# First batch, first token tile: the channel mixer's first product of four channel pairs with plain blocks and a relu from PSUM

## The chip, the cores and the metric

The kernel runs on one core of one Trainium2 chip. The metric is the device time of one launch in microseconds (us). The kernel before took 2399.0 us, the median of three runs from 2398.49 to 2399.86.

Engines by the names of the profile: PE is TensorE (PEld its weight loads), DVE is VectorE, ACT is ScalarE, POOL is GpSimd, SP is SyncE. SP, ACT and POOL also issue DMAs.

## What is computed

For x of shape (8, 3008, 256), float32: a global filter over the sequence, then a token mixer and a channel mixer.

```python
X = np.fft.rfft(x, axis=1)
x = np.fft.irfft(X * (filt_r + 1j * filt_i), n=3008, axis=1)
h = np.maximum(x.transpose(0, 2, 1) @ w_tok1, 0.0) @ w_tok2     # w_tok1 (3008, 256), w_tok2 (256, 3008)
u = x + h.transpose(0, 2, 1)
out = u + np.maximum(u @ w_ch1, 0.0) @ w_ch2                    # w_ch1 (256, 1536), w_ch2 (1536, 256)
```

The four mixer weights come as 64-bit floats; the kernel loads their words and makes float32 of them on the chip.

## The kernel before, in words

**Order of the work.** All is written out by hand: each engine executes its instructions in the order in which the Python code issues them. The transform of batch 0 comes first, then the token product of batch 0, then the mixer. `mix` goes through 288 items, one for each batch b, token tile m (six tiles of 512 tokens, the last of 448) and channel pair jp (six pairs of 2 x 128 hidden channels). Between the parts of an item, the main loop issues the steps of the next batch's transform. In items 0 to 5 (batch 0, tile 0) those are the first products of batch 1's transform (`a_unit`, L532, called x products in what follows), whose results are copied by ACT (L541) and stored to z_tmp by ACT's DMA queue (L543).

**One item, up.** "Up" is u @ w_ch1 for one pair: a product of a 2 x 2 block matrix of weights with a 2 x 2 block matrix of u (two halves of 128 input channels, two halves of 256 tokens). It is done with Strassen's method in Winograd's form: seven products of 128x128 weights with 256 columns instead of eight. `up_first` (L968 on) issues four of the seven (L973) into two PSUM banks "pg" and ACT copies the first result to s (L976). `up_middle` makes two sums on DVE: hh (128x256) and s (128x512), each with one input from PSUM. `up_last` issues the other three products (L989), makes two sums of 128x512 into hh on DVE, and ACT applies relu to hh in place (L994). All DVE sums go through the helper `v` and so have the line L951. The right-hand sums of u that the method needs are the tile v, made by `v_steps`.

**One item, down.** "Down" is relu(...) @ w_ch2 for the pair of the item before, again with seven products (`down`, L1007), accumulated over the six pairs in four PSUM banks "po". Its sums of hh are the tile t (`h_sums`: a 128x512 and two 128x256 sums). Part 0 of it uses hh, parts 1 and 2 use t.

**The weights.** The seven weight blocks of each pair lie in a tile wc: chan[0] for w_ch1, chan[1] for w_ch2. A loaded piece of 128x512 words (`wc1_load`, L392, four DMAs; `wc2_load`, L403, one DMA) is made float32 in steps: ACT L281, DVE L283 and L284, then DVE L287, L289 and the sum L316 into wc. These five DVE steps are called a convert. The raw blocks are then in four of the seven places, and `combine` (L377 to L384) makes the other sums in place with five 128x128 operations on POOL, L380 to L384. The converts of the last ten pieces (the list LAST) are spread over items 0 to 5, one or two an item: wc2 0, wc1 1, wc1 4, wc2 1, wc1 2, wc2 2, wc1 5, wc2 3, wc2 4, wc2 5. A wc1 piece serves two pairs for one half of the input channels; with its second half there, `wc1_load` combines the first pair of the two at once and puts the second off until the next wc2 piece. The list `stages` gives these pieces four buffers in turn, so a piece's load waits for the convert four pieces earlier.

**What else stands in the queues.** POOL, after the last combines, clears three filter tiles (L587) for batch 1's transform and, from item 4 on, stores the token weights' raw blocks (`w1_sums`, L796 and L797). SP loads batch 1's remaining rows of x, then reads z_tmp back (L659, L660) and loads the filters (L227 to L233); their product is L705 on DVE. ACT issues the stores of z_tmp. In item 3, two token units of the next tile (`u_unit`, L880 and L872) are issued on PE.

The lines above are those of the kernel before; the diff adds lines, so that in the kernel after they stand 2 to 20 lines further down.

Of the kernel before, what the change touches and what calls it, by code (L numbers as in the profile page):

```python
# [13 lines left out]
AF = mybir.ActivationFunctionType  # L14
# [30 lines left out]
DH = D // P  # L45
# [4 lines left out]
W2G = -(-N2 // NG)  # L50
PARTS = (0, 64, 96, 112)
BY_PE = 6
AP = A // 2
W1S = 7
IN_B = 16
# [73 lines left out]
def kernel(  # L129
# [11 lines left out]
    nc = tc.nc  # L141
# [41 lines left out]
    def bank(tag):  # L183
        return (psg if tag == "pg" else psum).tile([P, 512], FP32, tag=tag, name="ps_" + tag)
# [30 lines left out]
    chan = []  # L215
# [172 lines left out]
    def wc1_load(i, late=True):  # L388
        c, q = divmod(i, DC // 512)
        st = stage(512)  # L390
        for g in range(CB):
            nc.gpsimd.dma_start(st[ts(g, CW)], moe_w_ch1[ds((g * DH + c) * CW, CW), ts(q, 512)])  # L392
        yield

        yield from rounded(st, 512, [(lambda v: v.rearrange("p (i j n) -> p i j n", j=2, n=P),
                           chan[0][:, 2 * q:2 * q + 2, slice(0, 5, 4) if c == 0 else slice(1, 7, 5)])], late)
        if c == DH - 1:
            combine(chan[0][:, 2 * q:2 * q + 1])
            put_off.append(2 * q + 1)

# [568 lines left out]
    def up_first(jp, ut, vt, w, g):  # L969
        hw = w // 2  # L970
        for ps, n, mov in ((g[0][:, 0], 0, ut[:, 0, 0:hw]), (g[0][:, 1], 5, vt[:, 2, 0:hw]),
                           (g[1][:, 0], 6, vt[:, 0, 0:hw]), (g[1][:, 1], 4, vt[:, 1, 0:hw])):
            nc.tensor.matmul(ps[:, 0:hw], chan[0][:, jp, n, :], mov, start=True, stop=True)  # L973

        s = sp.tile([P, 3, 256], FP32, tag="s", name="s")[:, :, 0:hw]
        nc.scalar.copy(out=s[:, 0], in_=g[0][:, 0, 0:hw])  # L976
        return s

    def up_middle(hh, w, g, s):
        hw = w // 2  # L980
        u2 = hh[:, 2, 0:hw]
        v(u2, g[0][:, 1, 0:hw], s[:, 0])
        v(s[:, 1:3], g[1][:, :, 0:hw], u2.unsqueeze(1).to_broadcast([P, 2, hw]))

    def up_last(jp, ut, vt, w, g, s, hh):
        hw = w // 2
        for ps, n, mov in ((g[0][:, 0], 1, ut[:, 1, 0:hw]), (g[0][:, 1], 2, ut[:, 1, hw:w]),
                           (g[1][:, 1], 3, vt[:, 3, 0:hw])):
            nc.tensor.matmul(ps[:, 0:hw], chan[0][:, jp, n, :], mov, start=True, stop=True)  # L989
        h = hh[:, :, 0:hw]  # L990
        for i, add in enumerate((s[:, 0:2], s[:, 2].unsqueeze(1).to_broadcast([P, 2, hw]))):
            hs = h[:, 2 * i:2 * i + 2]
            v(hs, g[i][:, :, 0:hw], add)
            nc.scalar.activation(out=hs, in_=hs, func=AF.Relu)  # L994
# [103 lines left out]
    h1s, uts, vts = {}, {}, {}  # L1098
# [6 lines left out]
    def v_steps(b, m):  # L1105
        vts[b, m] = vp.tile([P, 4, 256], FP32, tag="v", name="v")
        t13, t2, t4_ = u_sums(uts[b, m], vts[b, m], width(m))

        def t24():
            t2()  # L1110
            t4_()

        return [t13, t24]

    todo_v = []
# [5 lines left out]
    def mix(next_ready):  # L1121

        wait = []
        pos, hhs, tts = {}, {}, {}

        def loads(b):
            if b + 1 < B and next_ready(b):
                for c in wait:
                    t4_load(b + 1, c)
                wait.clear()  # L1130


        own = ({(3, 0): (0,), (3, 2): (1,)}, {(2, 2): (0,), (3, 0): (1,), (3, 2): (2, 3)})
        new = {(JP - 2, 0): (0, 1), (JP - 1, 0): (2, 3)}

        def u_parts(b, m, jp, place):
            parts = own[b > 0] if m + 1 < MT else new if b + 1 < B else {}
            now = parts.get((jp, place), ())
            b, m = (b, m + 1) if m + 1 < MT else (b + 1, 0)
            for part in now:  # L1140
                u_part(b, m, part)
            if now and now[-1] == max(p for ps in parts.values() for p in ps):
                if m:
                    wait.append(m)
                todo_v.extend(v_steps(b, m))
                if b and (b, m) < (B - 1, MT - 2):
                    w2m_load((m + 2) % MT)

        to_dram = [f for m in range(MT) for f in w2_sums(m)]
        w1_todo, w1_out = w1_sums()  # L1150
        items = [(b, m, jp) for b in range(B) for m in range(MT) for jp in range(JP)]
        n = MT * JP
        for i in range(len(items) + 1):
            now, old = i < len(items), i >= 1
            if not now:
                bo, mo, jo = items[i - 1]
                t = tp.tile([P, 4, 256], FP32, tag="t", name="t")
                last_item(bo, mo, jo, hhs.pop(i - 1), t, uts[bo, mo], pos[bo, mo])
                break
            if i == JP - 2:  # L1160
                w1_todo.pop(0)()
            elif JP + 2 <= i and w1_todo:
                for _ in range(2):
                    w1_todo.pop(0)()
            elif i > JP + 2 and w1_out:
                w1_out.pop(0)()
            if i and ended[0] < len(tiles):
                convert_middle()
                convert_end(False)
                convert_middle()  # L1170
            if now:
                b, m, jp = items[i]
                if i % n == 0:
                    wait.append(0)
                w = width(m)
                hhs[i] = hp.tile([P, 4, 256], FP32, tag="hh", name="hh")
                g = [bank("pg").rearrange("p (s n) -> p s n", s=2) for _ in range(2)]
                s = up_first(jp, uts[b, m], vts[b, m], w, g)
                up_middle(hhs[i], w, g, s)
            while todo_h1:  # L1180
                todo_h1.pop()()
            if i < JP:
                one_step()
            if old:
                bo, mo, jo = items[i - 1]
                tts[i - 1] = tp.tile([P, 4, 256], FP32, tag="t", name="t")
                for f in h_sums(hhs[i - 1], tts[i - 1], width(mo)):
                    f()
                down(mo, jo, 0, hhs[i - 1], tts[i - 1], pos.setdefault((bo, mo), []))
            if now:  # L1190
                u_parts(b, m, jp, 0)
            copies()
            yield b, i % n, 0
            if ended[0] < len(tiles):
                if i == 0:
                    convert_middle()
                convert_end(False)
            if now:
                up_last(jp, uts[b, m], vts[b, m], w, g, s, hhs[i])
                if b + 1 < B and i % n == n - 4:  # L1200
                    t4_sums(b + 1, 0)
            one_step()
            if i >= JP:
                one_step()
            if now and b + 1 < B:
                if n - 4 - W1S <= i % n < n - 4:
                    w1_load(i % n - (n - 4 - W1S))
                if i % n == n - 4:
                    t4_sums(b + 1, 1)
            copies()  # L1210
            loads(b)
            yield b, i % n, 1
            if old:
                down(mo, jo, 1, hhs[i - 1], tts[i - 1], pos[bo, mo])
            yield b, i % n, 1.5
            if old:
                down(mo, jo, 2, hhs.pop(i - 1), tts.pop(i - 1), pos[bo, mo])
                if jo == JP - 1:
                    todo_v.extend(finish(bo, mo, uts[bo, mo], pos[bo, mo]))
                    one_step()  # L1220
                    one_step()
            if now:
                if b + 1 < B and i % n == n - 4:
                    h1s[b + 1] = yield from token_product(b + 1)
                u_parts(b, m, jp, 2)
                if jp == JP - 1:
                    while todo_v and m + 1 == MT:
                        one_step()
                if i >= 8 and to_dram:
                    to_dram.pop(0)()  # L1230
                if i in (28, 29):
                    w2m_load(i - 28)
            loads(b)
            yield b, i % n, 2
        while todo_v:
            one_step()

    with tc.manual_schedule():
# [45 lines left out]
        for i in range(IN_B, A // 2 + TC * W2G):  # L1284
            convert()
            if i == A // 2 + BY_PE - 1:
                sum_up()
# [4 lines left out]
        for dh in range(DH):  # L1292
            convert()
            u_part(0, 0, dh)
        for f in v_steps(0, 0):
            f()
        convert_end(False)
        for _ in range(XB):
            next(second)
# [8 lines left out]
        n = MT * JP  # L1308
        for b, i, place in mix(next_ready):
# [12 lines left out]
            jp = i % JP  # L1322
# [44 lines left out]
```

## Time and profile before

| | us |
|---|---|
| median of the timed runs | 2399.0 |
| the profiled execution's own time | 2400.86 |
| its span, from the first to the last instruction | 2399.1 |
| start of item 0's up on PE | 141.8 |
| start of item 4's up on PE | 184.7 |
| mean granted TensorE clock | 0.994 |

How to read it: a row of a timeline has the start and the length in us, the engine, the line, the operation, the tile written and the tiles read, their shapes, and how many instructions were merged; in square brackets stands how long the engine was idle before it, and what ended that. A row of the windows has the stretch, its length, and the busy time of PE, PEld, DVE, ACT and POOL, each with a count, then the granted clock, the DMA engines' share and GB/s. The chain of waits lists start, length, engine, tile and line.

### The profile page before, as it was taken

What the parts mean: (1) busy time and instruction counts of PE and PEld (TensorE: products, weight loads), DVE (VectorE), ACT (ScalarE), POOL (GpSimd) and SP (SyncE); (2) the same over time, 40 slices, a digit from 0 to 9 for tenths busy, and PEclk for the clock granted to TensorE, in tenths of its full rate; (3) what the DMA queues carried; (4) which work ended last, traced back from release to release, by engine and by line L of the source; (5) the groups of instructions that cost most, each with busy time, mean ns of one, the idle gap of its engine ahead of it and who ended that gap; (6) DMA issues with size and microseconds to landing.
All of it is one profiled execution on the core that took longest, in us unless ns stands there. A gap on an engine that the chain in (4) does not pass through costs nothing.

```text
span 2399.1 us, 37048 instructions
## 1 busy us (share of the span) xinstructions
PE 2360.7 (98%) x13132; PEld 2014.8 (84%) x13132; DVE 1949.3 (81%) x3669; ACT 689.8 (29%) x1339; POOL 639.8 (27%) x1124
## 2 busy tenths in 40 slices
PE   7989999999999999999999999999999999999998
PEld 4667788888898888988888888988889888898887
DVE  7798887788887888788887788788888788877786
ACT  5732232222223222232222222132222322212222
POOL 7475624211211121112112311221121112112121
PEclk8999999999999999999999999999999999999999
DMA  8864446333354333533345333533335433331100
GB/s 225 238 188 125 149 130 223 121 109 89 109 181 128 101 98 110 194 114 99 96 149 158 113 94 103 188 118 107 92 114 172 135 96 98 108 130 32 39 15 21
DMA packets 190423, 294.28 MB, mean 123 GB/s; under 512 B 34444, under 2 KB 124962, under 8 KB 190238
## 3 DMA queue, kind: packets, MB, share of 16 engines
q1 hardware_dynamic: 148750, 231.24, 31.1%
q0 software_dynamic: 34688, 53.83, 8.6%
q10 hardware_dynamic: 6800, 6.85, 0.9%
q8 instruction: 104, 1.70, 0.3%
q14 instruction: 81, 0.66, 0.1%
HBM read 209.06 MB, written 82.72 MB: 122 GB/s over the span
## 4 chain that ended last, share of the span: by engine, by line
PE 92%; DVE 3%; DMA 3%; issue 1%; ACT 1%; POOL 1%; SPq 0%; ACTq 0%; DVEq 0%; POOLq 0%
PE ps_po L1007 35%; PE ps_pg L973 19%; PE ps_pg L989 15%; PE ps_b L525 3%; PE ps_b L837 3%; PE ps_acc L894 3%; PE ps_pg L525 2%; PE ps_acc L837 2%; PE ps_b L894 2%; PE ps_acc L872 2%; PE ps_b L872 2%; PE ps_b L786 1%; DMA x<-in_x_dram 1%; DMA filt<-in_filt_i_dram 1%; PE ps_acc L880 1%
## 5 line engine op out<-in xcount | busy, mean ns | idle before, releaser
L1015 POOL DMA_DIRECT2D out_dram<-r x752 | 408.2, 550 | 1451.2 <-issue 864.2
L994 ACT ACTIVATE hh<-hh 128x512 f32<-128x512 f32 (+1 forms) x576 | 347.7, 621 | 1002.1 <-DVE hh L951 998.3
L951 DVE TENSOR_TENSOR hh<-ps_pg,s 128x512 f32<-128x512 f32 (+3 forms) x864 | 481.9, 585 | 166.2 <-ACT s L976 156.1
L1007 PE MATMUL ps_po<-t,wc 128*128 128x256 f32 (+1 forms) x2296 | 556.4, 379 | 0.7 <-DVE t L951 0.6
L1007 PEld LDWEIGHTS ps_po<-t,wc 128*128 128x128 f32 x2296 | 427.1, 190 | 91.4 <-issue 33.5
L973 PE MATMUL ps_pg<-v,wc 128*128 128x256 f32 (+1 forms) x1728 | 413.6, 375 | 0.7 <-POOL wc L383 0.7
L1007 PE MATMUL ps_po<-hh,wc 128*128 128x256 f32 (+1 forms) x1722 | 411.5, 375 | 0.6 <-POOL wc L384 0.6
L973 PEld LDWEIGHTS ps_pg<-v,wc 128*128 128x128 f32 x1728 | 328.8, 190 | 39.0 <-POOL wc L383 1.2
L1007 PEld LDWEIGHTS ps_po<-hh,wc 128*128 128x128 f32 x1722 | 326.9, 190 | 38.5 <-POOL wc L384 1.4
L989 PE MATMUL ps_pg<-u,wc 128*128 128x256 f32 (+1 forms) x1152 | 291.8, 376 | 2.1 <-DVE hh L951 2.0
L951 DVE TENSOR_TENSOR t<-t,hh 128x256 f32<-128x256 f32 (+1 forms) x576 | 246.3, 428 | 19.8
L989 PEld LDWEIGHTS ps_pg<-u,wc 128*128 128x128 f32 x1152 | 216.9, 190 | 33.7 <-DVE hh L951 7.8
L951 DVE TENSOR_TENSOR s<-ps_pg,hh 128x512 f32<-128x512 f32 (+1 forms) x288 | 196.0, 681 | 30.0
L976 ACT COPY s<-ps_pg 128x256 f32<-128x256 f32 (+1 forms) x288 | 105.9, 368 | 331.1 <-PE ps_pg L973 329.9
L951 DVE TENSOR_TENSOR t<-hh 128x512 f32<-128x512 f32 (+1 forms) x288 | 194.3, 675 | 0.6 <-ACT hh L994 0.6
L973 PE MATMUL ps_pg<-u,wc 128*128 128x256 f32 (+1 forms) x576 | 170.0, 377 | 4.2 <-DVE hh L951 4.2
L989 PE MATMUL ps_pg<-v,wc 128*128 128x256 f32 (+1 forms) x576 | 168.8, 375 | 0.0
L973 PEld LDWEIGHTS ps_pg<-u,wc 128*128 128x128 f32 x576 | 107.9, 190 | 20.6 <-DVE hh L951 8.1
L989 PEld LDWEIGHTS ps_pg<-v,wc 128*128 128x128 f32 x576 | 108.9, 190 | 12.9
L951 DVE TENSOR_TENSOR u<-ps_acc,u 128x256 f32<-128x256 f32 (+1 forms) x84 | 46.1, 549 | 73.0 <-PE ps_acc L894 50.5
L951 DVE TENSOR_TENSOR u<-ps_b,u 128x512 f32<-128x512 f32 (+2 forms) x126 | 74.4, 591 | 28.9 <-PE ps_b L894 26.7
L894 PE MATMUL ps_acc<-w 128*128 128x256 f32 (+1 forms) x336 | 85.2, 376 | 0.0
(164 smaller groups left out, 2684.8 us busy)
## 6 DMA issues: line engine op xcount, KB each, us to landing
w<-w_tmp SPq DMA_DIRECT2D x84, 448.0 KB
w<-w_tmp SPq DMA_DIRECT2D x35, 896.0 KB
out_dram<-r POOLq DMA_DIRECT2D x696, 32.0 KB, 3.5
g_tmp<-t SPq DMA_DIRECT2D x112, 192.0 KB
t<-g_tmp SPq DMA_DIRECT2D x42, 512.0 KB
t<-z_tmp SPq DMA_DIRECT2D x196, 96.0 KB
z_tmp<-t SPq DMA_DIRECT2D x72, 256.0 KB
wb<-wbi_t SPq DMA_DIRECT2D x56, 256.0 KB
```

What stands on the lines that cost most here:

```text
L525: nc.tensor.matmul(outs(i, j), stat(i, j), mov(i, j), start=True, stop=True)
L786: nc.tensor.matmul(acc[:, t, :], w1[:, a, ts(t, P)], t4[b, a // TC4][:, a % TC4, :], start=(a == 0 and t == 0), stop=(a == A - 1 and t == ...
L837: nc.tensor.matmul(ps[:, at], w[:, n], mov, start=(j == 0 and i in (0, 2)), stop=(j == AP - 1 and i >= 5))
L872: nc.tensor.matmul(ps[:, ds(q * P, n)], t4[b, c][:, r, ts(dh, P)], wai[:, 0:n], start=(first and q == 0), stop=(not first and q == 3))
L894: nc.tensor.matmul(ps[:, ds(j * hw, hw)], h1[:, n, :], w2m[m % 2][:, at, 0:hw], start=(i < 2 and j == 0), stop=(j == len(todo) - 1))
L951: nc.vector.tensor_tensor(out=out, in0=in0, in1=in1, op=op)
L973: nc.tensor.matmul(ps[:, 0:hw], chan[0][:, jp, n, :], mov, start=True, stop=True)
L976: nc.scalar.copy(out=s[:, 0], in_=g[0][:, 0, 0:hw])
L989: nc.tensor.matmul(ps[:, 0:hw], chan[0][:, jp, n, :], mov, start=True, stop=True)
L994: nc.scalar.activation(out=hs, in_=hs, func=AF.Relu)
L1007: nc.tensor.matmul(po[i][:, j, 0:hw], chan[1][:, jp, n, :], mov, start=(jp == 0 and first == 1), stop=(jp == JP - 1 and last == 1))
L1015: q.dma_start(bass.AP(tensor=ob.tensor, offset=ob.offset + row * D + g * cw, ap=[[N1 * D, 32], [D if h else -D, n], [1, cw]]), blocks[ts(g ...
```

## The change

In the first four items (batch 0, tile 0, pairs 0 to 3) up is done with plain blocks: four products of 128x128 raw weights with 512 columns (`up_plain`), and ACT's relu reads the two PSUM banks and writes hh: one instruction of 128x512 for the first bank, two of 128x256 for the second, whose two halves go to hh in reversed order. No v, no s and no sums on DVE are used there. The combines of pairs 0 to 3 of w_ch1 leave the converts and are issued one an item in items 1 to 4, each behind the up of that item. The two v steps of tile 0, which stood ahead of the mixer, become steps that item 0 takes one by one.

```diff
+PLAIN = 4
...
-        if c == DH - 1:
+        if c == DH - 1 and 2 * q >= PLAIN:
             combine(chan[0][:, 2 * q:2 * q + 1])
             put_off.append(2 * q + 1)
...
+    def up_plain(jp, ut, hh):
+        ps = [bank("pg") for _ in range(2)]
+        for dh in range(DH):
+            for i, n in enumerate(((0, 4), (1, 6))[dh]):
+                nc.tensor.matmul(ps[i], chan[0][:, jp, n, :], ut[:, dh, :], start=(dh == 0), stop=(dh == 1))
+        for i in range(2):
+            two = ps[i].rearrange("p (s n) -> p s n", s=2)
+            if i == 0:
+                nc.scalar.activation(out=hh[:, 0:2], in_=two, func=AF.Relu)
+            else:
+                for j in range(2):
+                    nc.scalar.activation(out=hh[:, 3 - j], in_=two[:, j], func=AF.Relu)
...
                 hhs[i] = hp.tile([P, 4, 256], FP32, tag="hh", name="hh")
-                g = [bank("pg").rearrange("p (s n) -> p s n", s=2) for _ in range(2)]
-                s = up_first(jp, uts[b, m], vts[b, m], w, g)
-                up_middle(hhs[i], w, g, s)
+                if i < PLAIN:
+                    up_plain(jp, uts[b, m], hhs[i])
+                else:
+                    g = [bank("pg").rearrange("p (s n) -> p s n", s=2) for _ in range(2)]
+                    s = up_first(jp, uts[b, m], vts[b, m], w, g)
+                    up_middle(hhs[i], w, g, s)
+                if 0 <= i - 1 < PLAIN:
+                    combine(chan[0][:, i - 1:i])
...
             if now:
-                up_last(jp, uts[b, m], vts[b, m], w, g, s, hhs[i])
+                if i >= PLAIN:
+                    up_last(jp, uts[b, m], vts[b, m], w, g, s, hhs[i])
...
-        for f in v_steps(0, 0):
-            f()
+        todo_v.extend(v_steps(0, 0))
```

## The prediction

> **What bounds the kernel now.** I read the page first, then the chain of work that ended last over the first 260 us, then the timeline of each engine from 138 to 216 us.
>
> ```profile
> span 2399.1 us, 37048 instructions
> PE 2360.7 (98%) x13132; PEld 2014.8 (84%) x13132; DVE 1949.3 (81%) x3669; ACT 689.8 (29%) x1339; POOL 639.8 (27%) x1124
> PE 92%; DVE 3%; DMA 3%; issue 1%; ACT 1%; POOL 1%; SPq 0%; ACTq 0%; DVEq 0%; POOLq 0%
> ```
>
> As a whole the kernel is bound by TensorE. The change sits in a short stretch that is not; its chain of waits is:
>
> ```profile
> 140.84 0.70 DVE v L951
> ...
> 149.40 1.28 DVE hh L951 x2
> ...
> 159.86 1.20 DVE hh L951 x2
> ...
> 173.77 1.13 PE ps_po L1007 x4
> 174.90 1.72 PE ps_acc L880 x4
> 176.61 0.89 PE ps_acc L872 x8
> ...
> 184.85 1.73 PE ps_pg L973 x8
> ```
>
> From 140.8 to 173.8 us the chain runs almost wholly on VectorE; then it passes to TensorE and stays there until item 4 (the fifth channel pair) starts at 184.7. The busy times of that stretch agree:
>
> ```profile
> 150.00:160.00 10.00, 9.72 (x32) 7.05 (x32) 9.59 (x19) 3.81 (x7) 9.09 (x18) 0.83 0.75 197
> sum 42.90, PE 37.05 PEld 25.25 DVE 41.18 ACT 16.48 POOL 34.08; mean PE 7.41 PEld 5.05 DVE 8.24 ACT 3.30 POOL 6.82
> ```
>
> The second row sums 141.8 to 184.7: VectorE is busy 41.2 of 42.9 us, GpSimd 34.1. TensorE's 37.1 is too high, as its rows show:
>
> ```profile
> 141.82 0.59 PE L973 MATMUL ps_pg<-u,wc 128*128 128x256 f32 x2
> 143.09 1.56 PE L973 MATMUL ps_pg<-v,wc 128*128 128x256 f32 x6 [0.67 <-POOL wc L383]
> 150.13 1.22 PE L973 MATMUL ps_pg<-u,wc 128*128 128x256 f32 x2 [2.35 <-DVE hh L951]
> 151.15 2.61 PE L973 MATMUL ps_pg<-v,wc 128*128 128x256 f32 x6
> 184.69 0.59 PE L973 MATMUL ps_pg<-u,wc 128*128 128x256 f32 x2
> ```
>
> Six passes took 2.61 us right after a stall, where six took 1.56 before (granted clock 0.83 in that window). Undisturbed prices come from the chain. Each float32 product is two records. L880: four records of 512 columns, 1.72 us, so 0.86 a product. L973: eight records of 256 columns, 1.73 us, so 0.4325 a product. A token u unit (L880 and L872) costs 1.72 + 0.89 = 2.61.
>
> TensorE's real work from 141.8 to 184.7, by the program's order: four ups of 7 products, three downs of 7, so 49 x 0.4325 = 21.2; eight products of the second batch's first transform (L532), 8 x 0.86 = 6.9; two u units, 5.2. Sum 33.3 of 42.9 us. **9.6 us are there to be won**, whatever the edit.
>
> **Part 1, TensorE.** Four products of 512 columns replace seven of 256: 3.44 against 3.02 us an item, 1.7 us more over four items. The work becomes 35.0 us, so item 4 cannot start before 141.8 + 35.0 = 176.8. The ceiling of the gain is 184.7 - 176.8 = 7.9 us. Item 0 no longer waits for GpSimd's combine (0.67 above): the raw blocks were converted ahead of VectorE's row at 140.84.
>
> **Part 2, VectorE.** The rows of one item, up to where the next begins:
>
> ```profile
> 159.78 1.28 DVE L951 TENSOR_TENSOR hh<-ps_pg,s 128x512 f32<-128x512 f32 x2
> 160.98 0.41 DVE L283 TENSOR_SCALAR both<-both 128x512 uint32<-128x512 uint32 x1
> 164.36 0.68 DVE L283 TENSOR_SCALAR both<-both 128x512 uint32<-128x512 uint32 x1
> 165.82 0.41 DVE L951 TENSOR_TENSOR hh<-ps_pg,s 128x256 f32<-128x256 f32 x1
> 166.34 0.69 DVE L951 TENSOR_TENSOR s<-ps_pg,hh 128x512 f32<-128x512 f32 x1
> 166.95 0.68 DVE L951 TENSOR_TENSOR t<-hh 128x512 f32<-128x512 f32 x1
> 171.52 0.41 DVE L283 TENSOR_SCALAR both<-both 128x512 uint32<-128x512 uint32 x1
> ```
>
> An item lasts 171.52 - 160.98 = 10.5 us. Gone are the pair of hh sums (159.78 to 160.98, 1.20), the first hh sum (165.82 to 166.34, 0.52) and the s sum (0.61): 2.3 us an item, 9.3 over four. What stays, two weight converts (the first from 160.98 to 164.36, 3.4) and the three t sums, takes 8.1 to 8.2. TensorE's own item is 3.44 + 3.02 + 1.72 = 8.2 us. The two are then level: VectorE stops being the bound but has nothing to spare. The two v steps move behind the convert in item 0; nobody reads v before item 4, so that costs nothing.
>
> **Part 3, ScalarE.** It gives up one copy and two relus an item, and takes one relu of 512 and two of 256 columns from PSUM. Nearest rows:
>
> ```profile
> 134.05 0.60 ACT L862 ACTIVATE h<-ps_b 128x512 f32<-128x512 f32 x1 [1.41 <-PE ps_b L786]
> 143.82 0.37 ACT L976 COPY s<-ps_pg 128x256 f32<-128x256 f32 x1 [1.15 <-PE ps_pg L973]
> ```
>
> 0.60 + 2 x 0.37 = 1.3 us, against 0.37 + 2 x 0.60 = 1.6 before. ScalarE is busy 16.5 of 42.9 us. New is a wait: these relus wait for TensorE, and behind them stand the first step of the next convert (L281) and the transform's copies. Up of item 0 ends at 141.8 + 3.44 = 145.2, its last two relus near 146.2, L281 near 147.0. VectorE, from 140.84 on, has its v steps and one convert ahead, and asks at about 146.8: 0.2 once. In later items L281 is done before VectorE asks.
>
> **Part 4, GpSimd.** The number of combines is the same, twelve, but c(0), the combine of pair 0, leaves its place ahead of item 0, and c(0) to c(3) now stand among those of the second weight matrix, which the downs wait for.
>
> ```profile
> 151.29 2.11 POOL L392 DMA_DIRECT2D st<-in_moe_w_ch_dram  x4
> 163.14 0.96 POOL L380 TENSOR_SCALAR wc<-wc 128x128 f32<-128x128 f32 x1
> 166.81 1.56 POOL L403 DMA_DIRECT2D st<-in_moe_w_ch_dram  x2
> 187.68 1.11 POOL L796 DMA_DIRECT2D w_tmp<-w  x1
> 188.78 1.03 POOL L797 DMA_DIRECT2D w_tmp<-w  x1
> 193.39 0.53 POOL L380 TENSOR_SCALAR wc<-wc 128x128 f32<-128x128 f32 x1
> 195.93 2.73 POOL L587 MEMSET filt<- 128x1024 f32 x3
> ```
>
> A combine lasted 3.7 us at the longest (163.14 to 166.81) and 2.5 at the shortest (193.39 to 195.93). In the new order GpSimd's queue goes: loads of the last w_ch1 tile once an earlier convert has let its buffer go (147.0 + 3.4, about 150.5), c(0), second-matrix combine 1, two loads, c(1), combine 2, one load, c(4), c(2), combine 3, c(5), the two stores of L796 and L797, combine 4, c(3), combine 5. That is 11 combines and 2.11 + 1.56 + 0.78 + 2.14 = 6.6 us of issue, with hardly a gap. With c us a combine, the last ends at 157.1 + 11c. TensorE reads it in item 6, in the second product of this row:
>
> ```profile
> 201.14 1.46 PE L1007 MATMUL ps_po<-hh,wc 128*128 128x256 f32 x6
> ```
>
> That product stands at 201.57; moved by 7.9 it stands at 193.7. So GpSimd is in time up to c = 3.3 us. The shortest, c = 2.5, costs nothing; the longest, 3.7, ends at 197.8 and costs 4.1. From 150 to 172 us all that VectorE does beside it reads SBUF, from 175 on it has gaps. I take 3.4, between the ends: 194.5, **0.8 late**. The earlier hand-overs are as tight: combine 1 at 150.5 + 2.1 + 2 x 3.4 = 159.4, against TensorE at 141.8 + 3 x 3.44 + 3.02 + 4 x 0.86 + 0.43 = 159.0; these 0.4 are part of the same 0.8.
>
> VectorE may pay too: L283 took 0.41 at 160.98 and 0.68 at 164.36. With 0.27 more on two of the four steps of a convert and half of it on the others, less what the item above already holds, an item is at most 1.3 us longer. The t sums that TensorE needs in item 3 at 171.5 would then come at 173.4 (169.6 otherwise). From nothing to 1.9; I take 0.5, as the converts of the stretch already lie beside combines.
>
> A rule of the Trainium skill speaks against the change: "SBUF — State Buffer", section "Who interferes with whom", says that a VectorE instruction with two SBUF inputs shuts out a GpSimd instruction that reads SBUF for its whole length, and that one with a PSUM input does not. The sums taken out are just those with a PSUM input. The sum by it is the slow rival below.
>
> **After item 4** every engine meets the same order as before, later waits included. One wait is not TensorE's:
>
> ```profile
> 202.91 0.33 SPq L227 DMA_DIRECT2D filt<-in_filt_r_dram  x1
> 213.63 1.22 DVE L705 TENSOR_TENSOR p<-ps_b,filt 128x1024 f32<-128x1024 f32 x1 [1.01 <-DMA filt<-in_filt_r_dram]
> ```
>
> The filter loads follow the second batch's last transform store, which moves with TensorE, and GpSimd's clearing of their tile (195.93). Moved by 6.6 us the first load would be issued at 196.3; the first clear ends at about 195.4. It just fits.
>
> **Sum.** 7.9 ceiling, less 0.8 for GpSimd and 0.5 for VectorE: 6.6 us. The profiled execution took 2400.86 us (1.8 outside its span), the median is 2399.0; the gain is the same on either. **Forecast 2392.4 us.**
>
> **Rivals.**
> - *GpSimd becomes the bound.* c = 3.7 and VectorE at half its upper price: 7.9 - 4.1 - 1.0 = 2.8, so 2396.2. For it: no gap in its queue for 44 us. Against: the 3.7 is already that of a combine beside a VectorE that was 96% busy (41.18 of 42.90).
> - *The gain is handed back at the filter loads.* If the clears stay where they were, the 1.01 us wait grows by up to the 6.6 won; 2396 to 2399.
> - *Slower: GpSimd locked out.* Each of a combine's five operations first waits for a whole VectorE instruction: 5 x (2.5/5 + 0.69) = 6.0 us a combine, the end at 157.1 + 66 = 223, 29 us behind 193.7; less 7.9 leaves 21 us lost, 2420. It breaks even at c = (201.6 - 157.1) / 11 = 4.0, and no combine so far took over 3.7. This is what that rule of the Trainium skill ("SBUF — State Buffer") gives if taken to its end; the trace has a combine of 3.7 us beside a full VectorE, so it bears it out only in part.
> - *The stalls simply stay* (the change does not do what it says): only if VectorE did not cause them; but TensorE's waits of 2.35 and 0.67 name the sums and the combine removed.
>
> **How the numbers follow.** Forecast, a gain of 5 to 8: 0.62. GpSimd as bound: 0.18. Handed back: 0.12. Locked out or another loss: 0.08. The range reaches down to the full 9.6 (2389.4), should the extra passes hide, and up through the second rival with VectorE at its full price (2397.3). 0.2% is 4.8 us, about what a measurement of this kernel can tell from no change: under 2394.2 counts as faster. Faster 0.62, within 0.30, slower 0.08.
>
> **What would show it.** In the changed profile: hh written by ScalarE from ps_pg twelve times; item 4's first up product near 177 to 178 instead of 184.7; TensorE without a stall over 1 us before that; VectorE's items about 8.2 us; GpSimd without gaps from 150 to 194 and combines of 3.2 to 3.6. Wrong if the combines pass 4 us, if item 4 starts after 181, or if item 4 is early and the time is not.

## The result and the profile after

The changed kernel takes **2396.07 us** (median of 22 runs, 2393.99 to 2399.17), the kernel before 2399.73 us beside it (22 runs, 2398.07 to 2402.78). The ratio is 0.9985 [0.9979, 0.9991]: 3.7 us faster, a real but small difference that lies within the 0.2% named in the prediction, so neither the forecast gain of 6.6 us came true nor "faster", which had been given 0.62. The profiled execution took 2395.43 us at a mean granted clock of 0.996.

The page of the kernel after, the same three lines as of before:

```profile
span 2393.7 us, 36991 instructions
PE 2356.6 (98%) x13108; PEld 2007.5 (84%) x13108; DVE 1943.6 (81%) x3653; ACT 688.1 (29%) x1339; POOL 641.0 (27%) x1124
PE 93%; DVE 3%; DMA 2%; issue 1%; POOL 1%; ACT 0%; SPq 0%; DVEq 0%; ACTq 0%; POOLq 0%
```

As a whole nothing looks different, so the stage has to be read by itself. TensorE's timeline of the kernel after, from item 0 to item 4:

```profile
139.77 3.60 PE L985 MATMUL ps_pg<-u,wc 128*128 128x512 f32 x8
...
149.64 1.02 PE L534 MATMUL ps_acc<-filt,wa 128*128 128x512 f32 x2
150.83 1.99 PE L1022 MATMUL ps_po<-t,wc 128*128 128x256 f32 x8 [0.16 <-DVE t L953]
...
156.95 0.59 PE L1022 MATMUL ps_po<-hh,wc 128*128 128x256 f32 x2
158.10 1.13 PE L1022 MATMUL ps_po<-hh,wc 128*128 128x256 f32 x4 [0.55 <-POOL wc L386]
...
167.10 1.13 PE L1022 MATMUL ps_po<-hh,wc 128*128 128x256 f32 x4 [0.57 <-POOL wc L386]
...
176.73 0.59 PE L975 MATMUL ps_pg<-u,wc 128*128 128x256 f32 x2
```

Item 0 starts at 139.77 here and at 141.82 before, which is not of the change's making: over the profiles of all kernels of this study, three of them without the change, it starts anywhere from 138.3 to 141.8. So times are counted from item 0. Item 4 follows 36.96 us behind it, against 42.87 before: **5.9 us are won in the stage**. The wait of 2.35 us for hh is gone; three short ones are left, for t (VectorE) and twice for a combine (GpSimd).

What becomes of the 5.9 us shows later, in the timelines of ACT, SP, DVE and PE of the kernel after: the last store of z_tmp, the first read of it, the first filter load, the product that needs the filters, and TensorE behind it.

```profile
186.76 0.33 ACTq L545 DMA_DIRECT2D z_tmp<-t  x1
...
193.65 0.30 SPq L661 DMA_DIRECT2D t<-z_tmp  x1
...
197.33 0.32 SPq L229 DMA_DIRECT2D filt<-in_filt_r_dram  x1
...
208.11 1.23 DVE L707 TENSOR_TENSOR p<-ps_b,filt 128x1024 f32<-128x1024 f32 x1 [2.90 <-DMA filt<-in_filt_r_dram]
...
210.85 1.13 PE L1004 MATMUL ps_pg<-u,wc 128*128 128x256 f32 x4 [2.67 <-DVE hh L953]
```

The same places of the kernel before, as far as the prediction has not shown them:

```profile
194.94 0.33 ACTq L543 DMA_DIRECT2D z_tmp<-t  x1
...
199.23 0.30 SPq L659 DMA_DIRECT2D t<-z_tmp  x1
...
216.37 1.13 PE L989 MATMUL ps_pg<-u,wc 128*128 128x256 f32 x4 [0.46 <-DVE hh L951]
```

The store is issued 8.2 us earlier, but its read follows 6.9 us behind it instead of 4.3. So the first filter load comes only 5.6 us earlier, VectorE waits 2.90 us for the filters instead of 1.01, the sum hh stands behind that wait, and TensorE waits 2.67 us for hh instead of 0.46. **2.2 us are given back there.** TensorE's records, matched one by one from the end, lie 8.0 to 8.2 us earlier than before through items 4 to 6, 7.7 at the start of item 8, 5.5 behind the wait at the filters, and 5.7 from 240 us to the last one; less the 2.05 of the earlier start, the profiles leave 3.6 us, the medians 3.7.

The step from 8.2 to 7.7 is a second, smaller loss ahead of the filters. There, in the timelines of VectorE and GpSimd after, lie:

```profile
194.61 1.66 DVE L953 TENSOR_TENSOR t<-t,hh 128x256 f32<-128x256 f32 x2
...
194.99 2.14 POOL L802 TENSOR_TENSOR w<-w 128x384 f32<-128x384 f32 x2
```

VectorE's two sums for t take 1.66 us beside GpSimd's sums of the token weights. In the kernel before they take 0.89 at 197.56, and GpSimd's sums start at 198.63, behind them. The 0.45 us fit that delay; no run tests it by itself.

What lies around the slow store shows in GpSimd's timeline of the kernel after:

```profile
181.45 1.11 POOL L798 DMA_DIRECT2D w_tmp<-w  x1
182.56 1.03 POOL L799 DMA_DIRECT2D w_tmp<-w  x1
...
192.29 2.73 POOL L589 MEMSET filt<- 128x1024 f32 x3
```

The DMA view of the kernel after from 178 to 212 us has each queue's packets, MB and share, then size and median us to landing by issue:

```profile
q0 software_dynamic: 608, 2.36, 22.2%
...
q10 hardware_dynamic: 432, 0.79, 6.2%
...
w_tmp<-w POOLq DMA_DIRECT2D x1, 1536.0 KB, 10.5
w_tmp<-w POOLq DMA_DIRECT2D x1, 768.0 KB, 5.5
```

And its window from 186 to 192 us, with the DMA engines' share and GB/s at the end:

```profile
186.00:192.00 6.00, 6.00 (x29) 5.13 (x28) 4.58 (x9) 2.06 (x5) 5.52 (x11) 1.00 0.90 308
```

The two stores of the token weights' raw blocks, 2.3 MB, move from 181.5 to about 192 and keep the DMA engines 0.90 busy; the 256 KB store of z_tmp at 186.76 falls into them. GpSimd's clears end at 195.0, two us ahead of the first filter load, so they are not what it waits for.

### The profile page after: what moved, and what is told of

It reads as the page before. It is cut to its first block, busy times and chain, and to the rows that moved or that the text cites. A ratio compares the mean times of both kernels' runs of the same rounds, so it can differ in the third digit from the quotient of the medians.

```text
span 2393.7 us, 36991 instructions
## 1 busy us (share of the span) xinstructions
PE 2356.6 (98%) x13108; PEld 2007.5 (84%) x13108; DVE 1943.6 (81%) x3653; ACT 688.1 (29%) x1339; POOL 641.0 (27%) x1124
## 4 chain that ended last, share of the span: by engine, by line
PE 93%; DVE 3%; DMA 2%; issue 1%; POOL 1%; ACT 0%; SPq 0%; DVEq 0%; ACTq 0%; POOLq 0%
PE ps_po L1022 35%; PE ps_pg L975 20%; PE ps_pg L1004 15%; PE ps_b L527 3%; PE ps_b L839 3%; PE ps_acc L896 3%; PE ps_pg L527 2%; PE ps_acc L839 2%; PE ps_b L896 2%; PE ps_acc L874 2%; PE ps_b L874 2%; DVE t L953 1%; PE ps_pg L666 1%; DMA x<-in_x_dram 1%; PE ps_b L680 1%
## 5 line engine op out<-in xcount | busy, mean ns | idle before, releaser
L1009 ACT ACTIVATE hh<-hh 128x512 f32<-128x512 f32 (+1 forms) x568 | 342.7, 621 | 989.1 <-DVE hh L953 989.1
L953 DVE TENSOR_TENSOR hh<-ps_pg,s 128x512 f32<-128x512 f32 (+3 forms) x852 | 475.4, 585 | 167.2 <-ACT s L978 157.1
L975 PE MATMUL ps_pg<-v,wc 128*128 128x256 f32 (+1 forms) x1704 | 406.6, 375 | 0.0
L975 PEld LDWEIGHTS ps_pg<-v,wc 128*128 128x128 f32 x1704 | 323.5, 190 | 36.9 <-DVE v L953 0.4
L1004 PE MATMUL ps_pg<-u,wc 128*128 128x256 f32 (+1 forms) x1136 | 287.7, 376 | 3.3 <-DVE hh L953 3.1
L975 PE MATMUL ps_pg<-u,wc 128*128 128x256 f32 (+1 forms) x568 | 166.9, 375 | 0.4 <-DVE hh L953 0.4
L1004 PE MATMUL ps_pg<-v,wc 128*128 128x256 f32 (+1 forms) x568 | 166.4, 375 | 0.0
L1004 PEld LDWEIGHTS ps_pg<-v,wc 128*128 128x128 f32 x568 | 107.3, 190 | 12.7
```

What stands on the lines that cost most here:

```text
L953: nc.vector.tensor_tensor(out=out, in0=in0, in1=in1, op=op)
```

## The experiments

Two questions were open. **Where do the 2.2 us go?** Theory A: into the collision of the z_tmp store with the two raw stores. Its rival, theory B: they go into something else, GpSimd's full queue above all, whose combines and clears come late wherever the stores stand. **Why were 5.9 us won?** Theory C: because VectorE has 2.3 us less to do an item. Rival D: because TensorE's up no longer waits for sums and combines, whatever VectorE's load. No experiment leaves out a part of the computation; e6 adds sums and e9 a store whose results nobody reads. Gains are against the kernel before in the same series (2399.09 to 2399.99 us).

**e1_store_item8** and **e1c_store_before**: the raw stores four items later in the program, on the kernel after and on the one before.

```diff
-            if i == JP - 2:
+            if i == JP + 2:
```

> The kernel after, with the two stores of the token weights' raw blocks (L798, L799) issued in item 8 instead of item 4. Theory A (the stores delay the transform's last z_tmp store, and so the filter loads): VectorE's wait for the filter at L707 falls from 2.90 us to 1 or less, TensorE's stall of 2.67 us behind it to 0.5 or less, and the kernel is 5.5 to 6 us faster than the kernel before instead of about 3.7. Theory B (the wait comes from GpSimd's clears or from the filter loads' own queue): the wait and the 3.7 us stay.

> The kernel before, with only that same move of the two stores to item 8. Theory A: there the wait was 1.01 us and TensorE's stall 0.46, so at most 0.5 us is to be had. Theory B: nothing. Either way within 0.5 us of the kernel before; if it is faster by 2 us or more, the move is worth something by itself and e1_store_item8 says nothing of the change.

Measured: e1 2400.86 us, 1.0005 [0.9996, 1.0014]; e1c 2405.57, 1.0028 [1.0017, 1.0038]. Both are slower than what they were made from. The timelines of GpSimd, ACT, SP and PE and the chain of waits of e1:

```profile
188.21 0.33 ACTq L545 DMA_DIRECT2D z_tmp<-t  x1
...
190.61 0.30 SPq L661 DMA_DIRECT2D t<-z_tmp  x1
...
194.57 1.11 POOL L798 DMA_DIRECT2D w_tmp<-w  x1
...
195.74 10.88 DMA filt<-in_filt_r_dram
...
213.63 1.42 PE L1004 MATMUL ps_pg<-u,wc 128*128 128x256 f32 x4 [4.14 <-DVE hh L953]
```

The z_tmp store now takes 2.4 us to its read, as A says. But GpSimd does not wait for item 8: it issues the stores as soon as its clears are done, 13 us later than before the move, and they fall on the filter loads, one of which lands after 10.88 us. TensorE waits 4.14 us. The expectation took the stores to be out of the way, and its number is missed. What stays is that the stores slow whatever short transfer of this chain they meet.

**e2_combines_late**: the combines of pairs 0 to 3, which nobody reads before the next token tile, behind the ups of items 5 to 8.

```diff
-                if 0 <= i - 1 < PLAIN:
-                    combine(chan[0][:, i - 1:i])
+                if 0 <= i - 5 < PLAIN:
+                    combine(chan[0][:, i - 5:i - 4])
```

> The kernel after, with the combines of pairs 0 to 3 issued in items 5 to 8 instead of 1 to 4, each just ahead of its first use; nothing else moved. Both theories: TensorE's two stalls of 0.55 and 0.57 us for GpSimd go, 1.1 us. Theory A: GpSimd reaches the two stores some 7 us earlier as well, the last z_tmp store no longer meets them, and 2.2 us more come back: about 7 us faster than the kernel before. Theory B: about 4.8.

Measured: 2391.46 us, 0.9966 [0.9953, 0.9978], **7.7 us faster than before**. From GpSimd's and TensorE's timelines of e2:

```profile
153.62 0.63 POOL L382 TENSOR_SCALAR wc<-wc 128x128 f32<-128x128 f32 x1 [2.66 <-DVE wc L318]
...
177.13 1.11 POOL L798 DMA_DIRECT2D w_tmp<-w  x1
...
207.34 1.13 PE L1004 MATMUL ps_pg<-u,wc 128*128 128x256 f32 x4 [1.24 <-DVE hh L953]
```

GpSimd now waits for VectorE's converts (2.66), and TensorE no longer waits for GpSimd in the stage. Item 4 comes 35.19 us behind item 0, without a stall: 1.77 better than after. The raw stores leave 4.3 us earlier, the z_tmp store (184.76, read at 190.14) takes 5.4 us instead of 6.9, and the later stall is 1.24 instead of 2.67. That is 1.8 + 1.4 = 3.2 of the 4.1 us by which e2's gain exceeds the change's. It does not part A from its rival: a relieved GpSimd also sends its stores earlier.

**e12_both**: e1 and e2 together.

> The kernel after with both moves, combines in items 5 to 8 and the two stores in item 8. Theory A: the two ways of freeing the z_tmp store don't add up, about 7 us faster than the kernel before, as e2_combines_late. Theory B: about 4.8.

Measured: 2393.33 us, 0.9975 [0.9966, 0.9985]: 1.9 us worse than e2 alone. The z_tmp store takes 2.7 us (184.48 to 187.19) and there is no wait at the filters at all. But the stores, now at 196.47 with only the last moved combine behind them, fall on the next filter loads: SP has issued these only at 210.1 us (205.3 in e5, below). TensorE's lead over before falls from 10.8 us at 215 us to 8.3 at 300; which wait brings that loss about was not followed. A later place seems only to move the collision.

**e5_late_and_store3** and **e5c_store3_before**: the raw stores one item earlier (`JP - 3`), on e2 and on the kernel before.

> The kernel after with the combines of pairs 0 to 3 in items 5 to 8 and the two stores L798 and L799 in item 3, where GpSimd now has room, so that their 2.3 MB have left before the last z_tmp store. Theory A (the stores' place against the chain z_tmp store, its read, filter loads): the z_tmp store takes 2.2 to 2.8 us to the first read of it instead of 5.4, VectorE's filter wait goes from 1.20 us to near 0, TensorE's stall of 1.24 goes: 8.5 to 9 us faster than the kernel before. Theory B (the remaining wait belongs to the filter loads): as e2_combines_late, 7.7.

> The kernel before with only the two stores moved to item 3. Theory A: the filter wait of 1.01 us and TensorE's 0.46 behind it go, at most 0.5 us faster; GpSimd's next combine is 2.1 us later there, where TensorE waited 0.28 for one, so up to 2 us slower is possible as well. If it were 3 us or more faster, the change's gain and that of the stores' place would have been mixed up.

Measured: e5 2391.29 us, 0.9967 [0.9955, 0.9978]; e5c 2399.62, 1.0001 [0.9992, 1.0010]. From ACT's, SP's and TensorE's timelines of e5:

```profile
158.21 2.00 PE L1022 MATMUL ps_po<-t,wc 128*128 128x256 f32 x8 [0.55 <-DVE t L953]
...
184.35 0.33 ACTq L545 DMA_DIRECT2D z_tmp<-t  x1
...
187.20 0.30 SPq L661 DMA_DIRECT2D t<-z_tmp  x1
```

The store takes 2.85 us and neither VectorE nor TensorE waits at the filters. But the stage is 0.8 us longer than in e2 (35.98 us, with a wait of 0.55 for t), so e5 equals e2 instead of beating it by the 1 us expected. On the kernel before the same move is worth nothing: the z_tmp store takes 2.1 us there and the 0.46 us of stall go, but about as much is lost ahead of them, where TensorE waits 1.06 us for hh in item 5 instead of 0.61.

**e8_store3**: that move alone on the kernel after, the direct test of A.

> The kernel after with only the two stores L798 and L799 moved to item 3; the combines stay in items 1 to 4. Theory A: the z_tmp store takes 2.2 to 2.8 us to its first read instead of 6.9, the filter wait falls from 2.90 us to 0.5 or less. Item 0 to item 4 gets 0 to 1.5 us longer, as the combine that TensorE needs in item 4 stands 2.1 us later on GpSimd. Net 4.5 to 6 us faster than the kernel before, against 3.7 of the kernel after. Theory B: no better than the kernel after, 2 to 3.7.

Measured: 2393.99 us, 0.9977 [0.9968, 0.9987], 5.5 us faster than before, as A expected. The clears are where they were in the kernel after (192.08); the stores leave earlier (167.91 instead of 181.45), and the combines between the two places come some 2 us later. The z_tmp store takes 2.84 us (186.92 to 189.76), VectorE does not wait for the filters any more, and TensorE's stall of 2.67 us behind that wait is gone. This speaks against the rival. The move has a price as well: TensorE waits 0.72 us for a combine in item 4. In its profiled execution about 1 us is lost at 198 to 203 us and 1.6 us at 235 to 243, in both places with VectorE's sums for t beside GpSimd's of the token weights (two of them take 2.24 and 2.90 us instead of 0.89); that was not followed further.

**e9_stores_doubled**: the other direction, on the kernel after.

```diff
+    w1x_d = nc.dram_tensor("w1x_tmp", (AP, P, 3, P), FP32, kind="Internal").ap()
...
+            more = w1x_d.rearrange("j p s n -> p j s n")
+            nc.gpsimd.dma_start(more[:, :, 0], w[:, :, 0, 0])
+            nc.gpsimd.dma_start(more[:, :, 1:3], w[:, :, 1])
```

> The kernel after with the two stores issued twice, the second time into a tensor of their own that nobody reads: 2.3 MB and 2.1 us of GpSimd more. Theory A: the last z_tmp store takes 11 to 14 us to its first read instead of 6.9, the filter wait grows from 2.90 to 8 to 10 us, and the kernel is 5 to 9 us slower than the kernel after. Theory B: only GpSimd's 2.1 us, 0 to 2 us slower than the kernel after.

Measured: 2403.16 us, 1.0016 [1.0006, 1.0025], 7.4 us worse in its gain than the change. Timelines of ACT, SP and PE of e9 (its lines stand up to 5 further down):

```profile
185.83 0.33 ACTq L547 DMA_DIRECT2D z_tmp<-t  x1
...
194.31 0.30 SPq L663 DMA_DIRECT2D t<-z_tmp  x1
...
214.12 2.07 PE L1009 MATMUL ps_pg<-u,wc 128*128 128x256 f32 x4 [5.49 <-DVE hh L958]
```

The store takes 8.5 us and the stall is 5.5. The direction and the size in time are A's; the store itself is less late than expected, and SP's issues behind it are slower too. With the stores away, once and twice, TensorE's stall behind the filters is nothing, 2.67 and 5.49 us: **A holds.**

**e6_sums_put_back**: the kernel after, with sums of the removed size given back to VectorE in items 0 to 3, from u into a tile that nobody reads.

```diff
...
+                    v(s[:, 2], u0[:, 0], u1[:, 0])
+                    v(s[:, 0:2], u0, u1)
...
+                    for _ in range(2):
+                        v(s[:, 0:2], u0, u1)
```

> The kernel after, with four VectorE sums (one of 128x256, three of 128x512, on u, into a tile nobody reads) put back into each of items 0 to 3, at the places of those that the change removed. They differ in having two SBUF inputs instead of one from PSUM. Theory C (the stage was won because VectorE lost 2.3 us an item): item 0 to item 4 on TensorE takes 42 to 45 us again instead of 37.0, and the time is that of the kernel before or 1 to 3 us over it. Theory D (it was won by leaving out the waits between VectorE and TensorE, u2 and s and the relu, whatever VectorE's load): the stage stays near 37 to 39.

Measured: 2402.62 us, 1.0012 [1.0003, 1.0022], 3.5 us slower than before. The sums take 1.1 + 1.4 = 2.5 us an item, and item 4 comes at 41.52 us: 4.6 of the 5.9 us are gone, though TensorE waits for no sum of up any more. (42 to 45 were expected. The stage is still 1.4 us shorter than before; that the whole is longer comes from behind it, where VectorE lags and TensorE waits 1.15 and 1.01 us for hh in items 4 and 5.) In its timeline it waits for t instead:

```profile
155.03 2.82 PE L1022 MATMUL ps_po<-t,wc 128*128 128x256 f32 x8 [2.31 <-DVE t L953]
```

So most of the gain is VectorE's time (C), and about 1.3 us the rest. These sums have two inputs in SBUF, the removed ones had one in PSUM, so the split is not exact.

**e7_plain6**: e5 with plain blocks for all six pairs (`PLAIN = 6`).

> As e5_late_and_store3, with plain blocks in all six items of the first tile instead of four (combines in items 5 to 10). Theory C: items 4 and 5 lie in a stretch where TensorE is the bound, so two more plain ups cost 2 x 0.43 us and win back only the 0.4 us that TensorE waits for VectorE at item 5: 0 to 1 us slower than e5_late_and_store3. Theory D: another 1 us or more faster.

Measured: 2397.34 us, 0.9993 [0.9984, 1.0001]. Up to 204 us TensorE is level with e5 counted from item 0 (both about 6.8 us ahead of before). Then, in its timeline:

```profile
227.41 2.93 PE L975 MATMUL ps_pg<-v,wc 128*128 128x256 f32 x6 [5.68 <-POOL wc L385]
```

The combine of a last pair stands in GpSimd's queue behind the stores of the first output tile and comes 5.68 us late. The stage says what C says (once TensorE is full, less work on VectorE brings nothing); the total is spoiled by the place of a combine.

**e10_plain2** and **e11_plain2_late**: plain blocks for two pairs only (`PLAIN = 2`), with the combines as in the change, and as in e2.

> The kernel after with plain blocks in items 0 and 1 only (combines of pairs 2 and 3 in the converts as in the kernel before). Theory C (2.3 us of VectorE an item): half of the stage's gain, item 0 to item 4 in 39 to 40.5 us instead of 42.9 and 37.0. Theory A on top: GpSimd reaches the two stores with less delay, so 0 to 1.5 us handed back: 1.5 to 3 us faster than the kernel before. Theory D: most of the stage's gain is in item 0's waits, so 38 or less.

> Plain blocks in items 0 and 1 only, as e10_plain2, but with the combines of pairs 0 and 1 in items 5 and 6, out of the way of the second matrix's combine that stalled TensorE for 5.82 us there. Theory C with GpSimd's order as the cause of that stall: it goes to 1 us or less, item 0 to item 4 takes 39 to 41 us instead of 45.3, and the kernel is 2.5 to 4.5 us faster than the kernel before. If the stall stays, plain blocks in two items cost GpSimd something other than the place of these two combines.

Measured: e10 2399.79 us, 1.0000 [0.9991, 1.0009]; e11 2395.53, 0.9982 [0.9973, 0.9991]. TensorE's largest stall in e10, from its timeline:

```profile
162.23 2.07 PE L1022 MATMUL ps_po<-hh,wc 128*128 128x256 f32 x4 [5.82 <-POOL wc L386]
```

And in e11:

```profile
158.78 1.13 PE L1022 MATMUL ps_po<-hh,wc 128*128 128x256 f32 x4 [3.18 <-POOL wc L386]
```

In e10 item 4 comes after 45.29 us, later than before, where 39 to 40.5 were expected: GpSimd's queue holds c(2), four loads and c(0) ahead of the combine that the down of item 1 needs, and TensorE waits 5.82 us for it. Without c(0) ahead, in e11, 3.18 us are left where 1 or less was expected. The stage takes 39.62 us, within the 39 to 41 expected, but with that stall in it, so it is no clean test of C. What the two show is that GpSimd's order decides what half the change brings.

The kernels whose stores were not moved in the program give A a scale, since GpSimd's queue shifts them against the z_tmp store:

| kernel | z_tmp store behind the first raw store, us | its read behind it, us |
|---|---|---|
| e10 | 9.6 | 3.5 |
| e11 | 8.2 | 4.6 |
| e2 | 7.6 | 5.4 |
| before | 7.3 | 4.3 |
| e6 | 7.3 | 5.2 |
| after | 5.3 | 6.9 |

The closer behind, the longer, by about as much, with 1 us of scatter.

## Why the prediction was right or wrong, step by step

- **9.6 us to be won, ceiling 7.9: right.** e2's stage has no stall and takes 35.19 us; 35.0 was the floor. The stage's own gain was 5.9 us where 6.6 were forecast.
- **Part 2, VectorE: the load right, the items not.** Items were to last 8.1 to 8.2 us. The first step of each item in VectorE's timeline after:

```profile
154.01 0.67 DVE L285 TENSOR_SCALAR both<-both 128x512 uint32<-128x512 uint32 x1
...
163.28 0.41 DVE L285 TENSOR_SCALAR both<-both 128x512 uint32<-128x512 uint32 x1
...
172.11 0.68 DVE L285 TENSOR_SCALAR both<-both 128x512 uint32<-128x512 uint32 x1
```

  They last 9.3 and 8.8 us, 0.6 to 1.1 more, within the upper price of 1.3. TensorE's direct loss is still small: t comes 0.33 us late once (TensorE's step at 149.64 lasts 0.86 and would be followed at 150.50; it is at 150.83), where 0.5 was taken. Part of the lateness reaches TensorE through GpSimd, in the next point.
- **Part 3, ScalarE: right.** The price was 1.3 us an item, the rows give 0.60 + 0.66 (two relus of 256 columns). The wait of 0.2 us, which its sum leaves out, did not come: VectorE begins the next convert at 146.05 without a gap.

```profile
142.54 0.60 ACT L989 ACTIVATE hh<-ps_pg 128x512 f32<-128x512 f32 x1 [1.93 <-PE ps_pg L985]
143.40 0.66 ACT L992 ACTIVATE hh<-ps_pg 128x256 f32<-128x256 f32 x2 [0.26 <-PE ps_pg L985]
```

- **Part 4, GpSimd: the size nearly right, the place wrong.** 0.8 us was to be lost at the last combine, with c = 3.4 and its end at 194.5. Combines after:

```profile
141.18 0.99 POOL L382 TENSOR_SCALAR wc<-wc 128x128 f32<-128x128 f32 x1 [1.96 <-DVE wc L318]
...
151.01 0.61 POOL L382 TENSOR_SCALAR wc<-wc 128x128 f32<-128x128 f32 x1
...
154.37 0.70 POOL L382 TENSOR_SCALAR wc<-wc 128x128 f32<-128x128 f32 x1
...
157.99 1.56 POOL L405 DMA_DIRECT2D st<-in_moe_w_ch_dram  x2
...
163.44 0.63 POOL L382 TENSOR_SCALAR wc<-wc 128x128 f32<-128x128 f32 x1 [0.71 <-DVE wc L318]
...
174.53 0.97 POOL L382 TENSOR_SCALAR wc<-wc 128x128 f32<-128x128 f32 x1
...
178.18 0.53 POOL L382 TENSOR_SCALAR wc<-wc 128x128 f32<-128x128 f32 x1
```

  The eleven of the sum take 3.0 to 3.7 us in the stage (3.36 from 151.01 to 154.37, then 3.62; 3.65 at 174.53) and 2.7 to 3.3 behind it; the last ends at 192.29 and nobody waits for it. The loss is at the first two hand-overs. TensorE's step at 158.10 would have come at 157.38 (156.95 + 0.43), so 0.72 late, for combine 1 (the prediction had 0.4). The one at 167.10 is 0.72 late as well: its combine had to wait 0.71 for VectorE's convert (row at 163.44). So 1.44 us hang on GpSimd, half of them through VectorE. 0.72 + 0.72 + 0.33 = 1.77 us, which is just what e2's stage is shorter; 0.8 + 0.5 = 1.3 had been taken.
- **"After item 4 every engine meets the same order as before ... It just fits": this step failed.** It took the filter loads to follow TensorE, held back at most by the clears. The way from the z_tmp store to its read was priced at its old 4.3 us, and it depends on what else the DMA engines move. The raw stores stand in GpSimd's queue, which the change fills; counted from item 0 they moved up 4.2 us (187.68 - 141.82 = 45.9 before, 181.45 - 139.77 = 41.7 after), the z_tmp store 6.1. So the store fell deeper into the 2.3 MB, which cost 2.6 us on the way and 2.2 on TensorE. e8 and e9 show it: with the stores away no stall, with them doubled 5.49. "Every engine meets the same order" left out a second thing: GpSimd's token-weight sums now lie beside VectorE's for t (0.45 us). With 7.9 - 1.8 for the combines and t, less 2.2 for the stores and 0.45 for these sums, 3.5 comes out; 3.7 was measured.
- **The rivals.** "Handed back at the filter loads" came true in part, 2.2 of 5.9 us, with another cause than the clears that it named. "GpSimd as the bound" had the right engine for the other loss, at about a third of its price (1.4 instead of 4.1 us). "Locked out" did not happen: one combine, the row at 141.18, took 4.2 us, over the 4.0 from which it decides, but it lies ahead of the eleven. The Trainium skill's rule behind it ("SBUF — State Buffer", section "Who interferes with whom") would give 6.0 us a combine if taken to its end; the rows of the eleven say 3.7 at most, beside a VectorE that was busy 35.6 of 36.9 us (the window of the kernel after from item 0 to item 4). Its distinction by where the inputs lie, which the prediction quotes, agrees with the traces, as the last section shows. The window:

```profile
139.80:176.70 36.90, 35.62 (x115) 20.06 (x114) 35.60 (x61) 15.20 (x30) 32.45 (x50) 1.00 0.65 195
```

- **"The stalls simply stay": refuted**, by the stage; e6 shows that it was VectorE's load, more than the waits that the rows name, that had held TensorE.
- **The signs and the chances.** Item 4 starts at 176.73, as early as the sign asked for (177 to 178), but that is luck: counted from item 0's 141.8 of before it would be 178.8. No stall over 1 us is left ahead of it, as said; VectorE's items are longer than the 8.2 us named. The sign of being wrong "if item 4 is early and the time is not" is the one that came. A gain of 5 to 8 us had 0.62 and did not come; the measured 2396.07 lies where the rivals were put, almost on the 2396.2 of "GpSimd becomes the bound", which is a coincidence, as most of the loss had another cause. The range held because its upper part had been left for GpSimd and VectorE, not for the stores. (That end adds up to 7.9 - 4.1 - 1.9 = 1.9 us, 2397.1; the 2397.3 that stands there needs ScalarE's 0.2 as well.)

The best version is e2, or e5 at the same time: 7.7 and 7.8 us faster than before (0.9966 [0.9953, 0.9978], 0.9967 [0.9955, 0.9978]), twice the change's own gain, by issuing the four combines where nothing waits for them.

## What to carry to other kernels

When a stage gets faster, go on along its consumers to the first transfer, and look at which other queue has a large transfer near it: the two move by different amounts, and a chain that "moves along" is only right if they move together. Work that is put off should go behind everything that has a reader soon, on its own engine's queue: here four combines that nobody needed yet cost half of what the change can win. A place in the program is no time on an engine that waits for nothing: the stores of e1 and e12 went out as soon as GpSimd was free, into the next short transfer.

## What was not expected of the hardware

A store of 256 KB took 2.1 to 2.9 us from its issue to the read that waits for it with the large stores away (e1, e1c, e5, e5c, e7, e8, e12), 3.5 to 6.9 with 2.3 MB sent on GpSimd's queue in the 5 to 10 us ahead of it (before, after, e2, e6, e10, e11), 8.5 with twice that; a filter load of at most 48 KB landed after 10.88 us beside them. The Trainium skill says that each DMA engine takes turns between the queues that have work, a packet at a time ("DMA: Bandwidth & Descriptors", section "Queues, rings and completion order"). An estimate by that rule, with the packets of the DMA view above (2.36 MB in 608 and 0.79 MB in 432, so 2.1 times larger on GpSimd's queue) and 308 GB/s: 2.1 x 256 KB more, 1.8 us, on top of 2.1 to 2.9, 3.9 to 4.7 us. The measured 6.9 and 8.5 are above it, so turns of these sizes alone do not explain the delay here; what does was not measured, and whether the view's packets are the rule's was not either.

VectorE and GpSimd slow each other, and it depends on where VectorE's inputs lie. Over all profiles of this study, up to 300 us: VectorE's sums for hh of 128x512, with one input in PSUM, took 0.67 to 0.69 us whether GpSimd worked beside them or not. Its sums for t of 128x256, with both inputs in SBUF, took 0.42 to 0.43 us in all 192 records with no GpSimd operation beside them, and 1.10 to 1.20 us in all 35 that met GpSimd's sums of 128x384 and nothing else; such a sum takes about 1.0 us itself, so there VectorE loses the better part of a whole GpSimd operation. Beside the short steps of a combine it is less, 0.42 to 0.72 us for the same sums. VectorE's convert steps of one input (128x512) took 0.40 to 0.43 us alone and 0.41 to 0.69 beside a combine. A combine of five operations took 2.5 to 4.4 us.
